# Sliding-window attention with a gated feed-forward: where the wide tiles transpose q and k, and which engine takes one of the x differences

## The chip, the cores and the metric

The kernel runs on one core of a Trainium2 chip. The metric is the device time of one execution in microseconds (us); lower is better. TensorE, VectorE (DVE in the profile), ScalarE (ACT), GpSimd (POOL) and SyncE (SP) each work through their own instructions in program order and wait for each other by semaphores.

## The reference

```
# q, k, v: [8, 8, 576, 64]   (batch, heads, positions, head size)
scores = q @ k^T / 8
keep   = (0 <= i - j) & (i - j < 64)            # causal window of 64 positions
attn   = softmax(where(keep, scores, -1e9))
x      = (attn @ v) as [4608, 512]              # tokens x (heads * 64)
out    = (max(x @ w_gate, 0) * (x @ w_val)) @ w_out    # w_gate, w_val 512 x 1536; w_out 1536 x 512
```

## The kernel before

The 4608 tokens are cut into ten tiles. Tiles 0 to 3 have 384 tokens, tiles 4 to 9 have 512 and are called wide. All matrix products run in fp16 with fp32 sums. The attention of a tile is computed while the feed-forward of the tiles before it runs.

**The order.** A planner (`Weaver`) keeps a clock that the code moves on with each group of TensorE products, and a heap of small steps with due times. `W.at(t, fn)` puts a step on the heap, and `W.advance` emits all steps that are due. This happens while the program is built: it decides the order of the instructions on every engine, and on the chip each engine then keeps that order. A step that waits on the chip holds up whatever stands behind it on its engine.

**q and k.** Each group of nine 64-position windows is one batch of q, k and v. The kernel loads q and k of a batch with four GpSimd DMAs (`qk_load`, L175: k and q, two groups of four heads each) and turns each with one VectorE transpose of 32 x 32 blocks (`qk_trans`, L195) into `kT` and `qT`. There are two sets of `kT` and `qT`, used in turn, and one buffer for each of the four loads, so a load waits until the transpose of the batch before has read its buffer. `plan_batch` puts the loads and the four transposes (k, k, q, q) on the heap. Of the wide tiles, 4 to 8 begin a new batch each and tile 9 does not.

**Scores and values.** The scores of a wide tile are computed in two quads of four windows (`q_st`, products at L261), each with four exponentials on ScalarE (`q_exp`, L402) and four masks on VectorE (`q_mask`, L407, fp16 in SBUF). `values` multiplies by v (L436), and VectorE divides by the sums (`t_recip` L450, `t_norm` L455) and turns the result into `xt` (`t_turn`, L461).

**The first two products of a wide tile** (`fast_hidden`, L597) use seven block products P1 to P7 in place of eight. They need four differences of blocks of x, called `xc`, made by `x_form` (L473): n = 0 needs only the first half of the heads, n = 1 needs the result of n = 0, n = 2 stands alone, and n = 3 needs n = 1. GpSimd makes n = 0, 2 and 3, VectorE makes n = 1:

```
x, y = ((b12, b11), (b22, xc[:, 0]), (b22, b12), (b21, xc[:, 1]))[n]
(nc.vector if n == 1 else nc.gpsimd).tensor_tensor(xc[:, n], x, y, SUB)
```

The 12 blocks of 128 hidden columns are taken in three groups, which the text calls blocks 0, 1 and 2. Within a block ScalarE copies sums out of PSUM (`seed` L606, `snap` L616). VectorE makes two kinds of work: the gate product of a direct result (`mult`, L622) and the sums of two results (`add`, L633), always one for the gate side and one for the value side. GpSimd multiplies the summed pairs (L622 on POOL). The product P3 writes on in the PSUM bank that the sum for P7 has read, so TensorE waits there for L633. Each block has two direct gates and two pairs of sums.

**What follows a tile's hidden part.** `fast_output` runs the third product (L699) in four groups of 128 tokens. Ahead of the first two stand the values of the next tile, ahead of the last two the scores of the tile after that. `o_sb` goes out by SyncE DMAs (L706).

**Where the transposes are planned.** `ahead(t)` runs at the beginning of each tile. In a wide tile t it plans the batch for tile t + 3, with times counted from the expected end of tile t (`T + WIDE_T`): loads 12 us earlier, transposes at `SLOTS` behind it, so they fall into tile t + 1. The batch for tile 6 is planned in tile 3 in the same manner.

Of the kernel before, what the change touches and what calls it, by code (L numbers as in the profile page):

```python
# [15 lines left out]
SUB = mybir.AluOpType.subtract  # L16
# [31 lines left out]
def kernel(  # L48
# [10 lines left out]
    nc = tc.nc  # L59
# [13 lines left out]
    NS = 4  # L73
# [69 lines left out]
    def xt_tile(t):  # L143
        if t not in xts:
            xts[t] = x_sb.tile([128, NC, WT], FP16, name="xt")
        return xts[t]
# [24 lines left out]
    def qk_load(b, name, hh):  # L171

        tile_ = nat[b, name, hh] = a_in.tile([128, S // 32 * D], FP16, name=f"{name}{hh}")
        src = (q if name == "q" else k)[b, G * hh:G * hh + G]
        nc.gpsimd.dma_start(tile_, src.rearrange("h (i j) d -> (h i) (j d)", i=32))  # L175
# [14 lines left out]
    def qk_trans(b, name, hh, j0=0, j1=S // 32):  # L190

        src = nat[b, name, hh].bitcast(FP32).rearrange("p (j e) -> p j e", e=32)
        dst = qTs[b % 2][:, hh] if name == "q" else kTs[b % 2][:, hh, 64:64 + S]
        dst = dst.bitcast(FP32).rearrange("p c o -> p (c o)")
        nc.vector.transpose(dst.rearrange("p (i j) -> p j i", i=32)[:, j0:j1], src[:, j0:j1])  # L195
# [36 lines left out]
    def one_bank():  # L232
        taken["one"] += 1
        to = singles[(taken["one"] - 1) % 4]
        while id(to) in unread:
            W.pop()
        return to

    def two_banks():
        taken["two"] += 1  # L240
        at = 4 + 2 * ((taken["two"] - 1) % 2)
        to = singles[at:at + 2]
        while any(id(one) in unread for one in to):
            W.pop()
        return to
# [141 lines left out]
    def q_window(qd, i):  # L387
        return NS * TT // 64 + QW * qd + i
# [21 lines left out]
    def scores(qd, T, banks=None, give=True):  # L410

        W.clock += q_st(qd, banks)
        for g in range(G):
            W.at(T + 0.8 + 0.6 * g, lambda g=g: q_exp(qd, g, give))
            W.at(T + 1.5 + 0.6 * g, lambda g=g: q_mask(qd, g))
# [50 lines left out]
    def x_form(t, n):  # L466

        if t not in xcs:
            xcs[t] = x_sb.tile([128, 4, 2, HT], FP16, name="xc", tag="xt")
        xt, xc = xt_tile(t), xcs[t]  # L470
        b11, b12, b21, b22 = (xt[:, 2 * k:2 * k + 2, HT * h:HT * h + HT] for k in range(2) for h in range(2))
        x, y = ((b12, b11), (b22, xc[:, 0]), (b22, b12), (b21, xc[:, 1]))[n]
        (nc.vector if n == 1 else nc.gpsimd).tensor_tensor(xc[:, n], x, y, SUB)  # L473
        if n == 3:
            normed[0] = t

    def values(t, hh, T, banks=None):

        t_pv(t, hh, banks or [bank() for _ in range(3)], banks is None)
        W.clock += 0.62  # L480
        W.at(T + 0.7, lambda: t_recip(t, hh))
        for i, k in enumerate((2, 0, 1)):
            W.at(T + 1.2 + 0.5 * i, lambda k=k: t_norm(t, hh, k))
        W.at(T + 2.7, lambda: t_turn(t, hh))
        for n, x in (((0, 4.0),), ((1, 4.0), (2, 4.1), (3, 5.0)))[hh]:
            W.at(T + x, lambda n=n: x_form(t, n))

    def w_form(wt, n, j):

        to = us if wt is wg else vs  # L490
        c = slice(256 * j, 256 * j + 256)
        f = slice(256 * j + 128 * HF, 256 * j + 128 * HF + 256)
        a11, a12, a21, a22 = wt[:, 0:2, c], wt[:, 2:4, c], wt[:, 0:2, f], wt[:, 2:4, f]
        x, y, op = ((a21, a22, ADD), (to[:, 0, :, c], a11, SUB), (a11, a21, SUB), (a12, to[:, 1, :, c], SUB))[n]
        nc.gpsimd.tensor_tensor(to[:, n, :, c], x, y, op)

    def plan_batch(b, load, trans):
        for i, (name, hh) in enumerate((n, hh) for n in "kq" for hh in range(2)):
            if load is not None:
                W.at(load, lambda name=name, hh=hh: qk_load(b, name, hh))  # L500
            W.at(trans[i], lambda name=name, hh=hh: qk_trans(b, name, hh))

    def plan_exps(T, u, mask=True, gap=0.4, first=0.8):
# [258 lines left out]
    with tc.manual_schedule():  # L762
# [85 lines left out]
        def pair(t, TA, TB, P):  # L848
            for u, T in ((2 * t, TA), (2 * t + 1, TB)):
                W.at(T, lambda u=u: u_st(u))  # L850
                plan_exps(T, u)
            W.at(P, lambda: u_pv(2 * t) + u_pv(2 * t + 1))
            for n in range(2):
                u = 2 * t + n
                W.at(P + 0.7 + 1.7 * n, lambda u=u: u_recip(u))
                for hh in range(2):
                    W.at(P + 0.9 + 0.5 * hh + 1.7 * n, lambda u=u, hh=hh: u_norm(u, hh))
                W.at(P + 1.9 + 1.7 * n, lambda u=u: u_turn(u))

        def loads(t, T):  # L860
            for u in (2 * t, 2 * t + 1):
                b, uu = divmod(u, UB)
                if uu == 0:
                    plan_batch(b, T - 12.0, (T - 1.5, T, T + 2.4, T + 4.8))
                W.at(T - 6.0, lambda u=u: v_load(u))
                W.at(T + 1.0, lambda u=u: v_spread(u))
# [5 lines left out]
        WIDE_T = L_T + 13.1  # L872

        def batch_of(t):
            w0 = q_window(2 * (t - NS), 0)
            b = (w0 + 2 * QW - 1) // NG
            return b, w0 <= NG * b

        def qk_ahead(t, T, gaps, lead=12.0):
            b, new = batch_of(t)  # L880
            if new:
                plan_batch(b, T - lead, [T + x for x in gaps])

        def v_ahead(t, T):
            b, new = batch_of(t)
            us = list(range(UB * b, UB * b + UB)) if new else []
            if t == NS:
                us.insert(0, UB * b - 1)
            for i, u in enumerate(us):
                W.at(T - 5.0, lambda u=u: v_load(u))  # L890
                W.at(T + 6.0 + 2.5 * i, lambda u=u: v_spread(u))

        LAST = NS + NL - 1
        SLOTS = (0.2, 3.4, 7.6, 13.8)

        def ahead(t):
            T = W.clock
            if t + 1 < NS:
                pair(t + 1, T + 8.5, T + 11.5, T + 17.3)
            if t == NS - 2:  # L900
                qk_ahead(NS, T + 20.5, (0.0, 1.5, 3.0, 4.5))
                v_ahead(NS, T + 20.0)
                for j in range(NF // 4):
                    for n, at in enumerate((0, 1, 3, 2)):
                        W.at(T + (1.0, 16.5, 22.9)[j] + 1.6 * n, lambda at=at, j=j: w_form(wv, at, j))
            if t == NS - 1:
                qk_ahead(NS + 1, T + 7.0, (0.0, 3.5, 4.7, 12.0), 6.0)
                for qd, x in ((0, 3.0), (1, 6.4), (2, 19.0), (3, 22.0)):
                    def st(qd=qd):
                        scores(qd, W.clock, two_banks() + two_banks(), qd == 3)  # L910
                    W.at(T + x, st)
                for hh in range(2):
                    def pv(hh=hh):
                        values(NS, hh, W.clock, two_banks() + [one_bank()])
                    W.at(T + 14.2 + 0.1 * hh, pv)
                qk_ahead(NS + 2, T + 27.6, SLOTS, 6.0)
                v_ahead(NS + 1, T + 27.6)
            if NS <= t:
                if t + 3 <= LAST:
                    qk_ahead(t + 3, T + WIDE_T, SLOTS)  # L920
                if t + 2 <= LAST:
                    v_ahead(t + 2, T + WIDE_T)

# [4 lines left out]
        T = 67.0  # L928
# [8 lines left out]
        for t in range(2, NS):  # L937
            ready(t)
            ahead(t)
            hidden(t, ((0, widths[t]),), each=4)  # L940
            output(t)
# [4 lines left out]
        for t in range(NS, NS + NL):  # L946
            ready(t)
            ahead(t)
            fast_hidden(t)
            between = [[] for _ in range(4)]  # L950
            if t + 1 <= LAST:
                between[0].append(lambda: values(t + 1, 0, W.clock))
                between[1].append(lambda: values(t + 1, 1, W.clock))
            if t + 2 <= LAST:
                for qh in range(2):
                    between[2 + qh].append(lambda qh=qh: scores(2 * (t + 2 - NS) + qh, W.clock))
            if t == LAST:
                fast_output(t, between[:-1])
                W.drain()
                output_last(t)  # L960
            else:
                fast_output(t, between)
# [31 lines left out]
```

## Time and profile before

| | |
|---|---|
| median of 3 runs | 318.36 us (318.19 to 318.55) |
| the profiled execution | 318.42 us |
| its span, first to last instruction | 316.7 us |
| TensorE busy | 302.8 us, 96% |
| VectorE busy | 225.6 us, 71% |
| ScalarE busy | 180.4 us, 57% |
| GpSimd busy | 160.5 us, 51% |
| granted TensorE clock | 1.00 |
| first wide tile (4) begins its products | 123.05 us |

In the profile, a group line gives the source line, engine, operation, result and inputs, shapes and count; behind the bar the busy time and the mean of one in ns, then the idle time of the engine just before and what ended it. A chain line gives a start, a length and a step. A timeline line gives a start, a length, the engine and the instructions merged into it; times in both are counted from the start of the span.

### The profile page before, as it was taken

What the parts mean: (1) busy time and instruction counts of PE and PEld (TensorE: products, weight loads), DVE (VectorE), ACT (ScalarE), POOL (GpSimd) and SP (SyncE); (2) the same over time, 40 slices, a digit from 0 to 9 for tenths busy, and PEclk for the clock granted to TensorE, in tenths of its full rate; (3) what the DMA queues carried; (4) which work ended last, traced back from release to release, by engine and by line L of the source; (5) the groups of instructions that cost most, each with busy time, mean ns of one, the idle gap of its engine ahead of it and who ended that gap; (6) DMA issues with size and microseconds to landing.
All of it is one profiled execution on the core that took longest, in us unless ns stands there. A gap on an engine that the chain in (4) does not pass through costs nothing.

```text
span 316.7 us, 10123 instructions
## 1 busy us (share of the span) xinstructions
PE 302.8 (96%) x4295; PEld 210.5 (66%) x4295; DVE 225.6 (71%) x413; ACT 180.4 (57%) x364; POOL 160.5 (51%) x178
## 2 busy tenths in 40 slices
PE   4899989999999998999999999999999999999995
PEld 2576947656646655885588458854887488748854
DVE  6937982787895886889876986699378937854540
ACT  3644324534526626882788267845885588518842
POOL 8859799513972019337814781347244404441430
PEclk9999999999999999999999999999999999999999
DMA  7999999929939216933990299002910210020002
GB/s 219 182 195 206 195 166 221 118 100 155 137 70 234 48 37 115 177 69 70 210 152 2 33 231 151 20 0 74 181 27 2 98 40 3 2 101 33 2 33 99
DMA packets 56748, 33.33 MB, mean 105 GB/s; under 512 B 39552, under 2 KB 48128, under 8 KB 56704
## 3 DMA queue, kind: packets, MB, share of 16 engines
q0 software_dynamic: 46688, 18.29, 49.8%
q1 hardware_dynamic: 9872, 14.34, 14.0%
q8 instruction: 33, 0.54, 0.7%
q14 instruction: 11, 0.09, 0.1%
q10 hardware_dynamic: 144, 0.07, 0.1%
HBM read 37.75 MB, written 9.44 MB: 149 GB/s over the span
## 4 chain that ended last, share of the span: by engine, by line
PE 84%; DVE 9%; ACT 3%; issue 1%; DMA 1%; POOL 0%; DVEq 0%; ACTq 0%
PE bank L597 30%; PE bank L699 19%; PE bank L554 19%; PE bank L714 7%; PE bank L261 3%; PE bank L436 2%; DVE kT L195 2%; DVE p L300 1%; PE bank L320 1%; DVE qT L195 1%; DMA vs<-in_k_dram 1%; DVE g_sb L622 1%; DVE pr L633 1%; PE bank L746 1%; ACT pr L616 1%
## 5 line engine op out<-in xcount | busy, mean ns | idle before, releaser
L622 POOL TENSOR_TENSOR g_sb<-pr 128x512 f16<-128x512 f32 x36 | 45.9, 1274 | 84.0 <-ACT pr L639 81.3
L699 PE MATMUL bank<-wo,g_sb 128*128 128x512 f16 x276 | 62.9, 380 | 0.0
L622 DVE TENSOR_TENSOR g_sb<-r,bank 128x512 f16<-128x512 f32 x36 | 24.7, 685 | 39.4 <-ACT r L650 25.8
L633 DVE TENSOR_TENSOR pr<-bank,pr 128x512 f32<-128x512 f32 x72 | 46.1, 680 | 2.4 <-PE bank L597 2.2
L616 ACT COPY pr<-bank 128x512 f32<-128x512 f32 x72 | 38.8, 595 | 11.8 <-PE bank L597 11.7
L699 PEld LDWEIGHTS <-g_sb 128*128 128x128 f16 x276 | 25.5, 98 | 28.9
L540 DVE TENSOR_TENSOR g_sb<-pr,bank 128x384 f16<-128x384 f32 x48 | 26.2, 549 | 22.0 <-PE bank L554 20.5
L537 ACT ACTIVATE pr<-bank 128x384 f32<-128x384 f32 x48 | 23.5, 494 | 24.8 <-PE bank L554 19.9
L554 PE MATMUL bank<-xt,wg 128*128 128x192 f16 (+1 forms) x256 | 34.8, 286 | 1.3 <-DVE xt L361 0.6
L201 POOL DMA_DIRECT2D v<-in_v_dram x41 | 34.7, 872 | 1.8 <-DMA q<-in_q_dram 1.0
L704 ACT COPY o_sb<-bank 128x512 f32<-128x512 f32 x23 | 13.5, 586 | 37.8 <-PE bank L699 32.3
L554 PE MATMUL bank<-xt,wv 128*128 128x192 f16 (+1 forms) x256 | 34.5, 286 | 0.0
L714 PE MATMUL bank<-wo,g_sb 128*128 128x512 f16 x144 | 32.8, 379 | 0.1
L597 PE MATMUL bank<-xc,us 128*128 128x256 f16 x216 | 32.4, 273 | 0.4 <-ACT pw L402 0.4
L597 PE MATMUL bank<-xc,vs 128*128 128x256 f16 x216 | 32.4, 273 | 0.3 <-ACT pw L402 0.3
L597 PEld LDWEIGHTS <-us 128*128 128x128 f16 x288 | 28.1, 98 | 6.7 <-issue 3.5
L597 PEld LDWEIGHTS <-vs 128*128 128x128 f16 x288 | 28.1, 98 | 4.6 <-issue 1.3
L473 POOL TENSOR_TENSOR xc<-xt 128x512 f16<-128x512 f16 x12 | 13.9, 1161 | 31.8 <-DVE xt L461 31.8
L554 PEld LDWEIGHTS <-wg 128*128 128x128 f16 x256 | 22.9, 98 | 10.3 <-DMA wg<-in_moe_w_gate_dram 0.8
L554 PEld LDWEIGHTS <-wv 128*128 128x128 f16 x256 | 22.8, 98 | 8.0
L639 ACT ACTIVATE pr<-pr 128x512 f32<-128x512 f32 x36 | 22.9, 636 | 7.7 <-DVE pr L633 7.7
L402 ACT ACTIVATE pw<-bank 128x512 f16<-128x512 f32 x48 | 25.4, 604 | 3.3 <-PE bank L261 2.9
(77 smaller groups left out, 481.3 us busy)
## 6 DMA issues: line engine op xcount, KB each, us to landing
out_dram<-o_sb SPq DMA_DIRECT2D x35, 256.0 KB, 3.3
k<-in_k_dram POOLq DMA_DIRECT2D x15, 288.0 KB, 5.4
q<-in_q_dram POOLq DMA_DIRECT2D x15, 288.0 KB, 7.8
v<-in_v_dram POOLq DMA_DIRECT2D x31, 128.0 KB, 6.5
v<-v SPq DMA_DIRECT2D x14, 132.0 KB, 3.3
v<-v SPq DMA_DIRECT2D x28, 66.0 KB, 3.0
wg<-in_moe_w_gate_dram POOLq DMA_DIRECT2D x6, 256.0 KB, 6.6
wv<-in_moe_w_val_dram POOLq DMA_DIRECT2D x6, 256.0 KB, 8.2
```

Of the source, the lines that this page charges most:

```text
L201: nc.gpsimd.dma_start(v16s[b % 2][lo:hi, g, :, 0:64], v[b, :, 64 * g - 64 + lo:64 * g - 64 + hi].rearrange("h p d -> p h d"))
L402: nc.scalar.activation(d["p"][g].rearrange("p n c -> p (n c)"), d["st"][g], ACT.Exp, scale=scale)
L537: nc.scalar.activation(part(r_sb), part(h1), ACT.Relu)
L540: nc.vector.tensor_tensor(g_sb[:, f:f + w, c0:c0 + n], part(r_sb), part(h2), MUL)
L554: nc.tensor.matmul(h[:, b * n:b * n + n], wt[:, c, (f + b) * 128:(f + b) * 128 + 128], xt[:, c, c0:c0 + n], start=(c == 0), stop=(c == NC ...
L597: nc.tensor.matmul(to[:, HT * m:HT * m + HT], w[:, k, 128 * m:128 * m + 128], x[:, k], start=(first and m == 0 and k == 0), stop=(k == 1), ...
L616: nc.scalar.copy(pr[:, i], at[j, "A", i])
L622: eng.tensor_tensor(gh[:, f:f + 2, h], pair(r), pair(v), MUL)
L633: nc.vector.tensor_tensor(pr[:, i], to, pr[:, i], ADD)
L639: nc.scalar.activation(pr[:, 0], pr[:, 0], ACT.Relu)
L699: nc.tensor.matmul(op, g_sb[:, f, 128 * sub:128 * sub + 128], wo[:, f], start=(i == 0), stop=(i == NF - 1))
L714: nc.tensor.matmul(op, g_sb[:, f, bass.ds(sub * 128, 128)], wo[:, f], start=(f == 0), stop=(f == NF - 1))
```

## The change

Three things are edited. First, all four differences of `x_form` are made by GpSimd. Second, the loads and the transposes of a batch are planned apart: `qk_loads` plans the loads at the time that they had before, and `qk_turns`, called at the beginning of wide tile t, plans the transposes of the batch for tile t + 2 from that tile's own beginning. Third, the offsets are new. Tiles 5 and 6 put both k transposes at the beginning, one q transpose behind the sums of block 0 and one behind those of block 1. Tile 4 has later offsets, so that its transposes stand at the beginning and behind the sums of blocks 0, 1 and 2, one at each place. The order of instructions on TensorE, ScalarE and SyncE stays as it was.

```diff
@@ x_form
-        (nc.vector if n == 1 else nc.gpsimd).tensor_tensor(xc[:, n], x, y, SUB)
+        nc.gpsimd.tensor_tensor(xc[:, n], x, y, SUB)
@@ plan_batch
             if load is not None:
                 W.at(load, lambda name=name, hh=hh: qk_load(b, name, hh))
+            if trans is None:
+                continue
             W.at(trans[i], lambda name=name, hh=hh: qk_trans(b, name, hh))
@@ ahead
-        SLOTS = (0.2, 3.4, 7.6, 13.8)
+        SLOTS = (0.1, 1.4, 8.0, 14.2)
+
+        def qk_loads(t, T):
+            b, new = batch_of(t)
+            if new:
+                plan_batch(b, T, None)
+
+        def qk_turns(t, T, slots=SLOTS):
+            b, new = batch_of(t)
+            if new:
+                plan_batch(b, None, [T + x for x in slots])
...
-                qk_ahead(NS + 2, T + 27.6, SLOTS, 6.0)
+                qk_loads(NS + 2, T + 21.6)
                 v_ahead(NS + 1, T + 27.6)
             if NS <= t:
+                if t + 2 <= LAST:
+                    qk_turns(t + 2, T, (3.6, 8.0, 14.2, 18.6) if t == NS else SLOTS)
                 if t + 3 <= LAST:
-                    qk_ahead(t + 3, T + WIDE_T, SLOTS)
+                    qk_loads(t + 3, T + WIDE_T - 12.0)
                 if t + 2 <= LAST:
                     v_ahead(t + 2, T + WIDE_T)
```

## The prediction

> **What bounds the kernel now.** I read the page first, then the chain that ended last in order of time, then the timeline of the wide tiles, then the groups of the instructions that the change moves.
>
> ```profile
> span 316.7 us, 10123 instructions
> PE 302.8 (96%) x4295; PEld 210.5 (66%) x4295; DVE 225.6 (71%) x413; ACT 180.4 (57%) x364; POOL 160.5 (51%) x178
> PE 84%; DVE 9%; ACT 3%; issue 1%; DMA 1%; POOL 0%; DVEq 0%; ACTq 0%
> ```
>
> TensorE is busy 96% of the span, so only TensorE's gaps can be won. VectorE (DVE) is the one other engine with a share of the chain that matters. Where DVE enters it, the chain in order of time tells:
>
> ```profile
> 160.37 0.69 DVE g_sb L622
> 161.06 1.17 DVE kT L195
> 162.23 0.53 DVE pr L633
> 162.76 0.04 issue
> 162.80 9.94 PE bank L597 x88
> ...
> 173.36 0.30 DVE qT L195
> 173.66 0.79 issue
> 174.45 0.69 DVE pr L633
> 175.15 0.04 issue
> 175.19 1.19 PE bank L597 x8
> ...
> 223.00 18.34 PE bank L597 x168
> ```
>
> This is wide tile 5. Twice a 1.25 us transpose of k or q (L195) stands in DVE's order between a gate product (L622) and the block's first sum (L633), and TensorE's product P3 (L597) waits for that sum. Tile 6 shows the same pair at 194.33 and 206.63. Tile 7, the last line, has no transposes, and its 168 products run without a step of another engine. The timeline gives the length of both stages, from the first product of the tile to the first values product (L436) of the next:
>
> ```profile
> 156.33 0.60 PE L597 MATMUL bank<-xt,wg 128*128 128x256 f16 x4
> ...
> 176.31 0.69 PE L436 MATMUL bank<-v,pw 128*32 128x65 f16 x64
> ```
>
> ```profile
> 222.84 0.60 PE L597 MATMUL bank<-xt,wg 128*128 128x256 f16 x4
> ...
> 241.27 0.69 PE L436 MATMUL bank<-v,pw 128*32 128x65 f16 x64
> ```
>
> Tile 5 takes 19.98 us, tile 6 (189.59 to 209.58) 19.99, tile 7 18.43. Tile 4 takes 19.93 (123.05 to 142.98), for partly other reasons. Last, the instructions that move:
>
> ```profile
> L195 DVE STREAM_TRANSPOSE kT<-k 128x576 f32<-128x576 f32 x16 | 19.7, 1243 | 0.2 <-ACT k L188 0.2
> L473 POOL TENSOR_TENSOR xc<-xt 128x512 f16<-128x512 f16 x12 | 13.9, 1161 | 31.8 <-DVE xt L461 31.8
> L473 DVE TENSOR_TENSOR xc<-xt,xc 128x512 f16<-128x512 f16 x6 | 8.4, 1403 | 0.7
> ```
>
> **The change, part by part.** TensorE, ScalarE and the DMA queue of SyncE keep their order; only DVE and GpSimd (POOL) change.
>
> *Tiles 5 and 6, transposes.* DVE's order was masks, k, gate, k, sum, sum ... gate, q, sum, sum. It becomes masks, k, k, gate, sum, sum, gate, sum, sum, q, gate and so on, with the second q behind the last sum of block 1. No transpose stands between a gate and its sums any more. That removes both gaps: 162.00 to 162.80 and on to 163.40, where 0.44 each is the undisturbed step, is 0.36 and 0.16; 173.88 to 175.19 and on to 175.78 is 0.87 and 0.16. The sum is 1.55, which is also 19.98 less 18.43. Tile 6 gives 1.56. Together 3.11 us.
>
> What hides them at the new places? The k pair follows the last mask (ends 156.37) and lasts 1.17 + 1.25, to 158.8. The gate behind it starts at 160.37, when ScalarE is done; DVE sat idle 2.84 us there. The first q keeps its place: in tile 7 the idle time there is 1.13 us (before 232.63), so at most 0.12 hangs over, and the sum behind it is ready 1.1 us before P3 asks (233.93 against 235.06). The second q goes where tile 7 shows DVE idle 1.76 us (before 238.75), which takes 1.25. If a cover were gone, the overhang beyond 0.59 us would reach TensorE: in tile 7 the sum ends at 228.32, P3 starts at 228.95, and 0.04 goes to the hand-over. Nothing else is late next, since tile 7 has no TensorE wait in this stage.
>
> *Tile 4, transposes.* The first k moves from between gate (128.07) and sum (129.93) to behind the last mask, the second k stays behind two sums, both q stand behind sums. TensorE's gap at that first sum goes: 129.76 to 130.50 and on to 131.10 is 0.30 and 0.16, together 0.46. The other gaps of tile 4, before 124.48 and 125.40, wait on ScalarE's exponentials; 1.03 us stays. But here k is loaded late, see the first rival.
>
> *The difference n = 1.* Six instructions of 1.40 us leave DVE, six go to GpSimd. GpSimd rows of this operation take 1.15 to 1.27; I take these ends, so GpSimd's chain n = 1, 2, 3 lasts 3.5 to 3.8 us. Before, it was 2.8 from the first difference behind the turn to the end of n = 3 (150.93 to 153.71). So everything behind it in GpSimd's queue comes 0.7 to 1.0 us later: the v loads behind four of the six chains and, in tile 4, four k and q loads ahead of them. The products that read the differences come much later: in tile 5 n = 3 ended at 153.71 and the first product with xc starts at 157.20. The v loads serve values some 20 us on. Cost on the path: nothing.
>
> On DVE the removal frees one thing on the path. In tile 4 the last q transpose of tile 5's batch waits behind this difference (118.80 to 120.17), and the scores at 121.40 wait 0.20 us for it. It will start at 118.66, behind the turn, and end by 119.9, before the scores begin at 120.32. They still stop at 120.80 for ScalarE. Gain 0.20, bounds 0 and 0.4.
>
> *Masks and GpSimd.* A mask takes 0.41 us, but the one that met the last GpSimd difference took 1.37: it waited until that was done. With three differences in a row there is more to meet. The strictest case is that GpSimd and the eight masks share no moment: 150.93 + 3 x 1.27 + 8 x 0.42 = 158.1 in tile 5 and 183.47 + 7.2 = 190.6 in tile 6. The k pair then ends at 160.5 and 193.1, against gates at 160.37 and 193.64: 0.15 late at most, inside the 0.59. The other end is no loss at all. I take nothing. [...]
>
> **Sum.** 3.11 + 0.46 + 0.20 = 3.77 us. The profiled execution took 318.42 (span 316.7 and 1.7 around it), so 314.65; it stands 0.06 above the median of 318.36, so 314.6.
>
> **Rivals.**
>
> *k lands late in tile 4 (other side).* The first k transpose of tile 4 now heads DVE's queue before the gate. Its load was issued at 121.35 and landed 4.1 us later; it will be issued at about 122.3 and land at 126.4, just before the last mask ends (126.6). Until 127.3 its start costs nothing (128.07 less 1.17 plus 0.59 less the 0.20 won above); from there each us is one on TensorE, since gate and sums queue behind it. Against it: the four k loads of tiles 4 and 5 landed in 4.1 to 6.5. For it: the q loads of the same queue took 7.8 to 9.4, and an output transfer and the v loads run beside it. At 6.5 the start is 128.8, 1.5 late, and the time 318.36 - 3.77 + 1.5 = 316.1. It decides from a landing of 8.8 (start 131.1); at 9.4 the start is 131.7, 4.4 late: 319.0.
>
> *GpSimd's DMA issues hold the masks too.* If the five v issues (4.3 us) behind the differences also kept masks out, the pair would come 3.7 us late in tile 5 and 3.0 in tile 6: 321.3; a third of that, 316.8. Against it: in tile 5 masks ran at 0.41 beside these issues.
>
> *The longer GpSimd chain reaches the products.* Six tiles with 0.7 to 1.0 more are 4.2 to 6.0, so 318.8 to 320.6. Against it are the 3.5 us of slack above; it decides only if a chain of 3.8 became one of 7. [...]
>
> *The gaps come back elsewhere.* If the transposes were only standing in for another wait of P3, the time would stay within 0.6 of 318.4. Against it is tile 7.
>
> *More is won.* If in tile 4 ScalarE's exponentials also fall into place, up to 1.03 more: 313.6.
>
> **Chances.** Forecast 0.72, with a range of its own of 314.0 to 315.3. Late k 0.08 at the partial size and 0.04 on the slower side. Held masks 0.06, at the partial size. Chain reaching the products 0.02. Gaps that come back 0.04. More won 0.04. This kernel's measurement can tell about 0.2% (0.64 us) from no change. Faster: 0.72 + 0.08 + 0.06 + 0.04 = 0.90; within 0.2%: 0.04; slower: 0.04 + 0.02 = 0.06. The range from 313.9 to 316.6 holds the forecast, most of the late k and a part of the held masks, and leaves out less than 0.2.
>
> **What would show it.** In the profile of the changed kernel, the stages of tiles 5 and 6 last 18.4 to 18.5 us, no chain step of L195 lies inside them, DVE's share of the chain falls by about 2 points, and GpSimd's L473 groups count 24 with 1.15 to 1.3 us each. In tile 4 the first k transpose starts by 127.3 less the shift and no wait on the sum is left. I am wrong if tiles 5 and 6 still show a TensorE gap before P3, if masks end after 158.7 in tile 5, or if DVE is found waiting for a DMA at the first k of tile 4.

## The result, and the profile after

| | before | changed |
|---|---|---|
| median, same chip | 318.46 us (4 runs) | 315.33 us (4 runs) |
| ratio | | 0.9904, 95% interval 0.9887 to 0.9921 |
| profiled execution | 318.42 us | 315.17 us |
| its span | 316.7 us | 313.5 us |

Forecast were 314.6 us, with a range of its own of 314.0 to 315.3, and 313.9 to 316.6 in all. The median lies inside the wide range and 0.03 us above the narrow one. The interval of the ratio stands for a gain of 2.5 to 3.6 us; the forecast gain of 3.77 us lies just outside it. In a second set of runs on another chip the changed kernel had a median of 314.96 us and a ratio of 0.9883 (0.9847 to 0.9919), a gain of 2.6 to 4.9 us, which holds the forecast. In what follows line numbers are those of the changed kernel: L599 is the wide tiles' product (L597 before), L624 the gate product (L622), L635 the sum (L633).

The page of the changed kernel, span, busy times and the shares of the chain that ended last:

```profile
span 313.5 us, 10122 instructions
PE 300.7 (96%) x4295; PEld 210.3 (67%) x4295; DVE 224.7 (72%) x407; ACT 180.1 (57%) x364; POOL 168.3 (54%) x184
PE 89%; DMA 3%; DVE 3%; ACT 2%; issue 1%; SPq 0%; DVEq 0%
```

VectorE lost six instructions and GpSimd won six, yet VectorE's busy time fell by only 0.9 us. Its share of the chain fell from 9% to 3%, where the prediction had about 2 points. The share does not measure the gain: from 100 us on, the steps of VectorE in the chain add up to 17.8 us before and to 0.6 us after, while the span fell by 3.2 us. Where TensorE waits, the chain goes back along the instructions of the engine that ended the wait, and those ran beside TensorE's products for the most part. In order of time, tiles 5, 6 and 7 now look the same in the chain:

```profile
156.36 18.34 PE bank L599 x168
...
188.08 18.34 PE bank L599 x168
...
219.77 18.34 PE bank L599 x168
```

All that TensorE's matmuls wait for from 100 us on, by what ended the wait (us in total, times, longest):

```profile
PE bank L599 <- ACT pw L402: 0.7, 2, 0.4
PE bank L261 <- ACT pw L402: 0.3, 1, 0.3
```

Before, this list had also 1.8 us on the sums and 0.2 us on the q transpose. Both lines are gone. The timeline shows where the k transposes went, in tile 4 and in tile 5:

```profile
127.68 1.26 DVE L195 STREAM_TRANSPOSE kT<-k 128x576 f32<-128x576 f32 x1 [0.81 <-DMA k<-in_k_dram]
...
128.78 0.68 DVE L624 TENSOR_TENSOR g_sb<-r,bank 128x512 f16<-128x512 f32 x1
...
129.39 1.27 DVE L635 TENSOR_TENSOR pr<-bank,pr 128x512 f32<-128x512 f32 x2
...
130.26 0.60 PE L599 MATMUL bank<-xt,us 128*128 128x256 f16 x4
...
150.77 5.56 DVE L407 TENSOR_TENSOR pw<-pw,mask 128x512 f16<-128x512 f16 x8 [0.28 <-ACT pw L402]
...
156.26 2.32 DVE L195 STREAM_TRANSPOSE kT<-k 128x576 f32<-128x576 f32 x2
...
160.24 0.69 DVE L624 TENSOR_TENSOR g_sb<-r,bank 128x512 f16<-128x512 f32 x1 [1.66 <-ACT r L652]
```

In tile 5 the pair ends at 158.6 and VectorE is idle for 1.66 us before the gate, as the prediction had it. In tile 4 VectorE did wait for k, 0.81 us. The prediction had named just this as a sign that it is wrong, and had asked for a start by 127.3 at the latest; it was 127.68. The first sum is done at about 130.1 all the same (the first half of the 1.27 us from 129.39), and P3 starts at 130.26 without a wait. So the sign came and the loss did not; the paragraph on the rivals tells why.

Where the 3.2 us of span came from, stage by stage. Each stage is a difference of two starts on TensorE, worked out from the trace of the one profiled execution of each kernel. Each ratio is to the kernel before on the same chip, which had medians of 318.46 to 319.09 us there, by fast runs alone. "Scores" reaches from the last scores ahead of tile 4 to its first product; "tile n" from a tile's first product to the next values product.

| kernel | scores | tile 4 | tile 5 | tile 6 | median | ratio to before (95%) |
|---|---|---|---|---|---|---|
| before | 2.73 | 19.93 | 19.98 | 19.99 | 318.46 | |
| changed | 2.37 | 19.47 | 18.43 | 18.43 | 315.33 | 0.9904 (0.9887 to 0.9921) |
| difference only | 2.37 | 19.92 | 19.98 | 19.99 | 318.40 | 0.9982 (0.9963 to 1.0001) |
| transposes only | 2.73 | 19.46 | 18.43 | 18.43 | 315.48 | 0.9897 (0.9867 to 0.9927) |
| k between again | 2.37 | 19.46 | 18.95 | 18.95 | 316.07 | 0.9907 (0.9882 to 0.9932) |
| q between again | 2.37 | 19.46 | 19.46 | 19.47 | 317.28 | 0.9947 (0.9927 to 0.9967) |
| k loads late | 2.37 | 27.59 | 18.43 | 18.43 | 322.64 | 1.0102 (1.0075 to 1.0128) |
| GpSimd reads | 2.37 | 19.46 | 20.10 | 19.38 | 317.43 | 0.9941 (0.9922 to 0.9960) |
| GpSimd writes | 2.38 | 19.46 | 18.43 | 18.43 | 315.39 | 0.9883 (0.9863 to 0.9903) |
| changed, again | 2.37 | 19.46 | 18.43 | 18.43 | 314.96 | 0.9883 (0.9847 to 0.9919) |
| early exponentials | 2.37 | 19.05 | 18.43 | 18.43 | 314.94 | 0.9876 (0.9844 to 0.9908) |
| ... and late copy | 2.37 | 18.95 | 18.43 | 18.43 | 314.32 | 0.9858 (0.9824 to 0.9891) |
| ... and early k | 2.37 | 18.43 | 18.43 | 18.43 | 313.96 | 0.9836 (0.9803 to 0.9869) |

A stage that no edit touches repeats to 0.01 us or so from kernel to kernel. The intervals of the ratios reach 0.5 to 1.2 us to each side, so smaller differences between two kernels are not told by the medians; the stages carry the readings below.

### The profile page after: what moved, and what is told of

The parts are those of the page before. It is cut to its first block, busy times and chain, and to the rows that moved or that the text cites. A ratio compares the mean times of both kernels' runs of the same rounds, so it can differ in the third digit from the quotient of the medians.

```text
span 313.5 us, 10122 instructions
## 1 busy us (share of the span) xinstructions
PE 300.7 (96%) x4295; PEld 210.3 (67%) x4295; DVE 224.7 (72%) x407; ACT 180.1 (57%) x364; POOL 168.3 (54%) x184
## 4 chain that ended last, share of the span: by engine, by line
PE 89%; DMA 3%; DVE 3%; ACT 2%; issue 1%; SPq 0%; DVEq 0%
PE bank L599 35%; PE bank L701 20%; PE bank L556 18%; PE bank L716 9%; PE bank L261 3%; PE bank L436 3%; DMA v<-v 2%; DVE qT L195 1%; PE bank L320 1%; DMA vs<-in_k_dram 1%; PE bank L748 1%; DVE kT L195 1%; DVE g_sb L542 1%; ACT pw L402 1%; ACT x L351 0%
## 5 line engine op out<-in xcount | busy, mean ns | idle before, releaser
L624 POOL TENSOR_TENSOR g_sb<-pr 128x512 f16<-128x512 f32 x36 | 45.9, 1275 | 73.3 <-ACT pr L641 72.6
L624 DVE TENSOR_TENSOR g_sb<-r,bank 128x512 f16<-128x512 f32 x36 | 24.8, 688 | 35.1 <-ACT r L652 24.2
L635 DVE TENSOR_TENSOR pr<-bank,pr 128x512 f32<-128x512 f32 x72 | 46.2, 683 | 2.9 <-PE bank L599 2.6
L407 DVE TENSOR_TENSOR pw<-pw,mask 128x512 f16<-128x512 f16 x48 | 29.2, 647 | 6.2 <-ACT pw L402 5.8
L599 PE MATMUL bank<-xc,us 128*128 128x256 f16 x216 | 32.4, 273 | 0.4 <-ACT pw L402 0.4
L599 PE MATMUL bank<-xc,vs 128*128 128x256 f16 x216 | 32.4, 273 | 0.3 <-ACT pw L402 0.3
L599 PEld LDWEIGHTS <-us 128*128 128x128 f16 x288 | 28.1, 98 | 3.9 <-issue 0.6
L599 PEld LDWEIGHTS <-vs 128*128 128x128 f16 x288 | 28.2, 98 | 3.8 <-issue 0.5
L473 POOL TENSOR_TENSOR xc<-xt 128x512 f16<-128x512 f16 x12 | 14.8, 1233 | 24.9 <-DVE xt L461 24.5
```

Source lines behind the costliest of these rows:

```text
L407: nc.vector.tensor_tensor(d["p"][g], d["p"][g], mask[:, None, :].to_broadcast([128, 2 * QW, 64]), MUL)
L599: nc.tensor.matmul(to[:, HT * m:HT * m + HT], w[:, k, 128 * m:128 * m + 128], x[:, k], start=(first and m == 0 and k == 0), stop=(k == 1), ...
L624: eng.tensor_tensor(gh[:, f:f + 2, h], pair(r), pair(v), MUL)
L635: nc.vector.tensor_tensor(pr[:, i], to, pr[:, i], ADD)
```

## The experiments

### Each half of the change alone

Difference only: the kernel before, with the one line of `x_form`.

```diff
-        (nc.vector if n == 1 else nc.gpsimd).tensor_tensor(xc[:, n], x, y, SUB)
+        nc.gpsimd.tensor_tensor(xc[:, n], x, y, SUB)
```

> The kernel before with only the x difference n = 1 moved to GpSimd; the transposes stay planned as before. My theory (the gain is made of separate gaps): only the gap at the scores of tile 4 goes, 0.2 to 0.4 us, so about 318.1; tiles 5 and 6 stay at 19.9 to 20.0 us, tile 4 keeps its waits on the sum. Rival (the freed DVE time carries the gain): 2 us or more faster, 316.4 or less. Rival (GpSimd is too slow for it): slower than 318.4 by 0.6 or more.

The scores stage fell by 0.36 us and no other stage moved. The median alone would not tell this from nothing (the interval ends at 1.0001). TensorE's waits from 118 to 212 us in this kernel:

```profile
PE bank L597 <- DVE pr L633: 1.8, 4, 0.7
PE bank L597 <- ACT pw L402: 0.7, 2, 0.4
PE bank L261 <- ACT pw L402: 0.3, 1, 0.3
```

All four waits on the sum are there still; only that on the q transpose is gone. The 8.4 us of VectorE time that the difference had taken bought 0.36 us.

Much of those 8.4 us was itself a wait for GpSimd, by an estimate from the next two lines and the masks. In the kernel before, VectorE's n = 1 started 0.02 us behind GpSimd's n = 2 and ended 0.28 us behind it, here for tile 5:

```profile
150.93 1.15 POOL L473 TENSOR_TENSOR xc<-xt 128x512 f16<-128x512 f16 x1 [0.78 <-DVE xt L461]
150.95 1.41 DVE L473 TENSOR_TENSOR xc<-xt,xc 128x512 f16<-128x512 f16 x1
```

A mask of the same size and with two inputs takes 0.41 us where it meets no difference. So, by this estimate, the change moved such a wait from n = 1 to the masks more than it freed VectorE; what n = 1 would take there alone, no run shows.

Transposes only: the changed kernel, with that line taken back.

> The changed kernel with n = 1 back on VectorE; only the transposes are planned anew. My theory: all gaps at the sums go (0.46 in tile 4, 1.55 each in tiles 5 and 6), the gap at tile 4's scores stays, so 0.2 to 0.4 slower than the changed kernel, 3.2 to 3.5 faster than before: about 315.0 to 315.6. In tile 4 the first k transpose starts about 1 us sooner than in the changed kernel (k is issued sooner). Rival (the transposes fit only because the difference left VectorE): the k pair ends behind the gate's time and half of the gain or more is lost, 316.9 or more.

The other share, to the hundredth: 2.73 us at the scores again, 18.43 in tiles 5 and 6, 19.46 in tile 4. So the k pair fits with the difference on VectorE too, and the rival that it does not falls. In tile 4 k had landed, and its first transpose started at 127.29 without a wait, though this run was 0.5 us later than the changed kernel at the tile's first product (123.62 against 123.11). The two halves are independent and add up.

### Which place costs what

The changed kernel, with one offset each.

```diff
-        SLOTS = (0.1, 1.4, 8.0, 14.2)
+        SLOTS = (0.1, 4.4, 8.0, 14.2)        # k between again
```

> The changed kernel with one offset changed, so that in tiles 5 and 6 the second k transpose stands between the first gate and the first sum again, as before. My theory: the first gap of each tile (0.36 and 0.16 on P3) comes back and nothing else: 1.0 us slower than the changed kernel, about 316.3; tiles 5 and 6 take 18.95. Rival (only the sum of transposes in a tile counts, not their place): same as the changed kernel, 315.3.

```diff
-        SLOTS = (0.1, 1.4, 8.0, 14.2)
+        SLOTS = (0.1, 1.4, 8.0, 15.8)        # q between again
```

> The changed kernel with one offset changed, so that in tiles 5 and 6 the second q transpose stands between the gate and the first sum of block 2, as before. My theory: the second gap of each tile (0.87 and 0.16) comes back: 2.1 us slower than the changed kernel, about 317.4; tiles 5 and 6 take 19.46. Rival (place does not matter): 315.3.

18.95 and 19.46 us, as forecast: 0.52 for the k transpose between gate and sum, 1.03 for the q transpose, twice each. The number of transposes in a tile is the same in all these kernels. In the medians of this set, against the kernel with GpSimd writes below (315.39 us, both tiles at 18.43), the two are 0.7 and 1.9 us slower, for 1.0 and 2.1 by the stages; the first of these is not clear of noise. In the second kernel the timeline of tile 5 shows the mechanism again:

```profile
172.33 1.25 DVE L195 STREAM_TRANSPOSE qT<-q 128x576 f32<-128x576 f32 x1
...
173.42 1.27 DVE L635 TENSOR_TENSOR pr<-bank,pr 128x512 f32<-128x512 f32 x2
...
174.16 0.60 PE L599 MATMUL bank<-xt,us 128*128 128x256 f16 x4 [0.71 <-DVE pr L635]
```

### The rival on the other side: k lands late in tile 4

The changed kernel, with the v loads ahead of the k and q loads in GpSimd's queue, in tile 4 alone.

```diff
-                qk_loads(NS + 2, T + 21.6)
                 v_ahead(NS + 1, T + 27.6)
+                W.at(T + 22.6, lambda: qk_loads(NS + 2, T + 22.6))
```

> The changed kernel with one thing moved: in tile 4 GpSimd issues the five v loads ahead of the four k and q loads, so k is issued about 4.2 us later. My theory: the first k transpose heads VectorE's queue, so beyond 127.8 us each us of its start is one on TensorE; k issued at 127.2 lands at 131.3 to 133.7, so the loss against the changed kernel is 3.5 to 5.9 us: 318.7 to 321.1, the whole gain or more. Rival (the block's work hides a late k, or the loads of k overtake): less than 1 us lost, below 316.4.

```profile
133.93 1.25 DVE L195 STREAM_TRANSPOSE kT<-k 128x576 f32<-128x576 f32 x1 [6.76 <-DMA k<-in_k_dram]
135.03 0.68 DVE L624 TENSOR_TENSOR g_sb<-r,bank 128x512 f16<-128x512 f32 x1
135.63 1.27 DVE L635 TENSOR_TENSOR pr<-bank,pr 128x512 f32<-128x512 f32 x2
...
136.36 1.01 PE L599 MATMUL bank<-xt,us 128*128 128x256 f16 x4 [5.63 <-DVE pr L635]
137.16 1.06 PE L599 MATMUL bank<-xt,vs 128*128 128x256 f16 x4
```

The mechanism is real: k, issued at 127.46, landed 6.4 us later, VectorE stood still for 6.76 us and TensorE for 5.63. This kernel is slower than the one before the change, ratio 1.0102. But tile 4 lost 8.1 us, not 3.5 to 5.9 (in the profiled execution, 323.35 us, the longest of the six). The rest comes after the wait. The next line gives a stretch and its length, the busy time of TensorE's matmuls, its weight loads, VectorE, ScalarE and GpSimd, then the clock that TensorE was granted, the share of the DMA engines and GB/s:

```profile
136.00:141.00 5.00, 4.64 (x22) 3.19 (x22) 4.04 (x6) 3.02 (x7) 1.26 (x1) 0.50 0.47 121
```

The granted clock was 0.50. As a sum, with 0.44 us for an undisturbed step of four products: 130.13 to 136.36 is 6.23 less 0.44, so 5.79 for the wait, and 136.36 to 141.31 is 4.95 for six steps of 0.44, so 2.3 for the clock. Together 8.1.

### Masks and GpSimd take turns

The changed kernel, with GpSimd instructions added behind n = 3 for tiles 5 and 6, once such as read SBUF (the engines' working memory), once such as only write it. Both write a tile that nobody reads any more.

```diff
         if n == 3:
             normed[0] = t
+        if n == 3 and t in (NS + 1, NS + 2):
+            for _ in range(4):                                    # GpSimd reads
+                nc.gpsimd.tensor_tensor(zero.rearrange("p (a n) -> p a n", a=2), b22, b12, SUB)
...
+            for _ in range(7):                                    # GpSimd writes
+                nc.gpsimd.memset(zero32.bitcast(FP16), 0.0)
```

> The changed kernel with four more differences on GpSimd into an unused tile, behind n = 3 for tiles 5 and 6 (about 5.3 us each; they add work, the result is the same). My theory (GpSimd instructions that read SBUF and masks take turns, one by one): four more masks take 1.3 us each, the k pair starts at about 160.2 in tile 5 and 191.1 in tile 6, the gate is 2.3 and 1.4 late, less 0.59 each: 2.5 us slower than the changed kernel, about 317.8. Rival (masks are held only by the first GpSimd instruction, or the pair's cover is larger): less than 0.5 slower. Rival (the later v loads are what costs): slower by the same amount as the next run.

> The changed kernel with seven fills on GpSimd at the same place in place of the four differences (they write SBUF and read nothing; 4 to 6 us for each tile, estimated from the fills of 64 and 128 columns that took 0.18 and 0.23 us). [...] Rival (any GpSimd work holds masks): about 2.5 slower, as in the run before.

VectorE in tile 5, first with the reads, then with the writes; and GpSimd with the writes:

```profile
150.60 9.40 DVE L407 TENSOR_TENSOR pw<-pw,mask 128x512 f16<-128x512 f16 x8 [0.29 <-ACT pw L402]
159.92 2.32 DVE L195 STREAM_TRANSPOSE kT<-k 128x576 f32<-128x576 f32 x2
162.09 0.67 DVE L627 TENSOR_TENSOR g_sb<-r,bank 128x512 f16<-128x512 f32 x1
```

```profile
151.39 5.75 DVE L407 TENSOR_TENSOR pw<-pw,mask 128x512 f16<-128x512 f16 x8 [0.28 <-ACT pw L402]
157.06 2.33 DVE L195 STREAM_TRANSPOSE kT<-k 128x576 f32<-128x576 f32 x2
```

```profile
154.94 5.50 POOL L478 MEMSET zero<- 128x768 f16 x7
```

With reads the eight masks last 9.40 us, the pair starts at 159.92, the gate is late, and tiles 5 and 6 lose 1.67 and 0.95 us, forecast 1.7 and 0.8. With 5.50 us of writes at the same place the masks last 5.75 us against 5.56 in the changed kernel, and both tiles stay at 18.43. So the four differences, which read SBUF, held the masks, and the seven fills, which only write it, did not. It is not GpSimd's time and not the v loads, which come later by about as much in both; the rival that any GpSimd work holds masks falls. The traces show the manner: one instruction of each engine in turn. In the changed kernel the masks of tile 5 range as follows (shortest, median and longest in ns):

```profile
L407 DVE TENSOR_TENSOR pw<-pw,mask x8: 414/416/1372, 150.8 to 155.9; 128x512 f16<-128x512 f16 x8
```

Three of the eight met a difference. They and the next one started 1.22 to 1.30 us apart; the last five started about 0.33 us apart.

### What is left of tile 4

The prediction kept 1.03 us of tile 4's gaps, on ScalarE's exponentials. Edits of ScalarE's order were tried on the changed kernel, which ran again beside them.

> The changed kernel again, unedited, beside the two versions below. Theory: 315.0 to 315.8. It also tells whether two places of its profile that are later than in the kernel before (0.40 us at the values products of tile 1 at 45 us, 0.24 at the second scores behind tile 4) come again (then they belong to the change) or not (then they vary from run to run).

The first place did come again. From the output products ahead of the values products of tile 1 to those behind them it is 5.45 us in the kernel before, 5.81 in the first profile of the changed one and 6.06 in this one. But all kernels of this study have the same program up to that point, and they range from 5.31 to 6.06 there, so it varies from run to run and does not belong to the change. It is a wait on the v spread (SyncE's transfer from v to v, L213) and on masks. The second place did not come again: the second scores behind tile 4 took 0.64 us as in the kernel before (0.87 in the first profile). That is a pause inside the products, put down to "issue": 0.49 us in the next run, nothing in most. Its cause is open.

```diff
-            W.at(T + 0.8 + 0.6 * g, lambda g=g: q_exp(qd, g, give))
+            W.at(T + 0.8 + gap * g, lambda g=g: q_exp(qd, g, give))      # gap: 0.1 in quad 3, else 0.6
```

> The changed kernel with the four exponentials of tile 5's second quad planned 0.1 apart in place of 0.6, so that on ScalarE they stand ahead of the copy of tile 3's last output, which waits for TensorE. Theory: in tile 4 the products before 124.5 and 125.5 wait for banks that these exponentials free; they go, but the first snapshot copy is about 0.4 late in their place: 0.5 us faster than the changed kernel, 314.8. Rival (the snapshot copies are the real limit there): no change, 315.3.

Tile 4 fell to 19.05 us, 0.41 of the 0.5 forecast. The median does not show it (314.94 against 314.96). The profiled execution had the pause of 0.49 us behind tile 4; whether the other executions had it is not known.

```diff
-        W.at(W.clock, evac)
+        W.at(W.clock + (2.0 if t == NS - 1 and sub == TT // 128 - 1 else 0.0), evac)
```

> As the run before, and the copy of tile 3's last output is planned 2 us later, so that on ScalarE it stands behind the two first snapshot copies. Theory: both gaps of tile 4 go, 0.9 us faster than the changed kernel: 314.4. Rival (the snapshots wait for something else): as the run before.

The time came out as forecast, 314.32 us for 314.4, but by luck: the changed kernel had 314.96 us in this set and not 315.3, so 0.64 us were won and not 0.9, and tile 4 shows 0.51 of it. The waits of tile 4's products on ScalarE are gone, and now the late k decides:

```profile
126.65 1.26 DVE L195 STREAM_TRANSPOSE kT<-k 128x576 f32<-128x576 f32 x1 [2.19 <-DMA k<-in_k_dram]
...
129.07 0.60 PE L599 MATMUL bank<-xt,us 128*128 128x256 f16 x4 [0.20 <-DVE pr L635]
```

Tile 4 takes 18.95, which is 18.43 and the 0.52 that a k transpose ahead of the first sum cost before. So the k loads were put ahead of the x differences, where GpSimd had been idle for 20 us:

```diff
-                qk_loads(NS + 2, T + 21.6)
+                b6 = batch_of(NS + 2)[0]
+                for name, at in (("k", 12.0), ("q", 21.6)):
+                    for hh in range(2):
+                        W.at(T + at, lambda name=name, hh=hh: qk_load(b6, name, hh))
```

> As the version with early exponentials and the late copy, and the two k loads of tile 6's batch stand ahead of the x differences on GpSimd (they were behind them), so that k has landed before tile 4 begins. In the run before, the first k transpose of tile 4 waited 2.19 us for its load and the first sum made TensorE wait 0.20 and 0.16 on P3. Theory: that wait goes, tile 4 takes 18.43 to 18.5 us (18.95 in the run before, 19.47 in the changed kernel): 0.5 us faster than the run before, about 313.8. Rival (the gap at the first sum has another cause): as the run before, 314.3.

```profile
119.66 4.93 DVE L407 TENSOR_TENSOR pw<-pw,mask 128x512 f16<-128x512 f16 x8
124.50 1.25 DVE L195 STREAM_TRANSPOSE kT<-k 128x576 f32<-128x576 f32 x1
126.72 0.69 DVE L624 TENSOR_TENSOR g_sb<-r,bank 128x512 f16<-128x512 f32 x1 [0.97 <-ACT r L652]
```

The transpose starts behind the last mask and is done a microsecond before the gate. Tile 4 takes 18.43 us like all others, and the only wait of a matmul that the profile names from 100 us on is 0.3 us at the scores ahead of tile 4. At 313.96 us, ratio 0.9836 (0.9803 to 0.9869), this version is faster than the kernel before. Against the changed kernel the stage shows 1.03 us; the interval of the ratio lies below that of the first set (0.9887 to 0.9921) and overlaps that of the second (0.9847 to 0.9919), and the two kernels were not run on one chip together.

## Why the prediction was right

**Tiles 5 and 6.** 3.11 us forecast, 1.55 and 1.56 measured. That the place makes the cost, and not the number, is shown by the two runs that put one transpose back: 0.52 and 1.03, the two terms of the sum. The covers held: 1.66 us idle are left before the gate of tile 5.

**Tile 4's sums.** 0.46 forecast, 0.46 measured (19.93 to 19.47).

**The q transpose at the scores.** 0.20 forecast with bounds 0 and 0.4, 0.36 measured, alone by the difference-only run. The term was too small because only the wait with a name was counted. Before, the scores stopped twice, at 120.80 for ScalarE and at 121.40 for the transpose; after, they stop once and run on from 121.22 in one piece. Besides the named wait of 0.20 us the second start is saved, 0.16 us. First the kernel before, then the changed one:

```profile
120.80 0.39 PE L261 MATMUL bank<-qT,kT 32*128 32x64 f16 x29 [0.28 <-ACT pw L402]
121.40 0.42 PE L261 MATMUL bank<-qT,kT 32*128 32x64 f16 x32 [0.20 <-DVE qT L195]
```

```profile
121.22 0.66 PE L261 MATMUL bank<-qT,kT 32*128 32x64 f16 x61 [0.27 <-ACT pw L402]
```

**The x difference.** 3.5 to 3.8 us were forecast for GpSimd's three differences; in tile 4 they took 3.75 (119.25 to 123.00). TensorE waited for none of them, as forecast. VectorE did wait, for the k loads that stand behind them in tile 4. VectorE was not freed by the whole 8.4 us: the masks of most tiles now meet two or three differences where they met one or none, and their busy time rose by 6.7 us (22.5 to 29.2). In tile 5 this cost nothing, since the masks catch up: they start 0.33 us apart and the exponentials ahead of them 0.48, and the k pair started at 156.26 against 156.29 before. The strictest case of the prediction, 158.1 for the end of the masks there, was too late by 1.8 us (it was 156.34): mask and difference together take 1.30 us, not 1.27 and 0.42, and masks in a row start 0.33 us apart, not 0.42. A difference took GpSimd 1.16 us where no mask ran (at 118.02), and a mask of that size took VectorE 0.41 where no difference ran, a factor of 2.8.

**The sum.** 3.77 us forecast; the four terms measured make 0.36 + 0.46 + 1.55 + 1.56 = 3.93. The profiled executions differ by 3.25, as the two places that vary from run to run happened to be 0.40 and 0.23 us longer in the changed kernel's. By the ratio, 3.77 in 318.4 is 0.9882; the two sets gave 0.9904 and 0.9883. That the second is so near to the forecast is chance, at an interval of 0.0036 to each side; what speaks for the sum are its four terms.

**The rivals.** The late k was near. The forecast had it issued at about 122.3 and landed at 126.4; it was issued at 122.95, landed 4.6 us later, and the transpose waited until 127.68. In the kernel without the difference on GpSimd it did not wait, so the wait is a cost of that part of the change. The limit of 127.3 was too strict by about 0.5, since 127.68 cost nothing and left 0.2. About half of this is the 0.20 that was taken off for an earlier tile, while the tile in fact began 0.06 later than before. The other half is a shorter way from transpose to sum: the gate started 1.10 us behind the transpose and the sum 0.61 behind the gate, for which the prediction had 1.17 and, by tile 7, 0.76. The prediction had not counted this cover, so that the late k cost nothing is in part luck. A us for a us beyond the limit was too low a price with k loads late: 8.1 us were lost there, 2.3 of them at a granted clock of 0.50. The forecast of 319.0 for the worst case counts the wait alone; what the clock does behind a wait of that length, no run shows. Held masks by DMA issues: refuted, masks ran at 0.41 beside them (154.58 to 156.34). (The price of that rival, 3.7 and 3.0 us, is 0.1 and 0.2 too low by the prediction's own rows: with the masks 4.3 us later the pairs end at 164.8 and 197.4, against gates at 160.37 and 193.64 and less 0.59 that is 3.8 and 3.2. It decided nothing.) The chain reaching the products, and the gaps coming back: refuted by 18.43. More won in tile 4: not by this change, but by the two edits of ScalarE's order and the early k loads.

## What to carry to other kernels

A step that is not urgent should stand behind the last instruction of a pair that somebody waits for, not between its two halves: the same 1.25 us cost 1.03, 0.52 or nothing by place alone, and a tile without the step shows where the idle time is to put it. Ahead of an in-order engine's queue such a step brings its own input onto the path, so look at where its load lands, and load earlier if another engine's queue delays the issue. Moving work off an engine is worth what waits behind it at that place (0.36 us here), not its busy time (8.4 us).

## What the runs showed of the hardware

With k loads late, TensorE ran at a granted clock of 0.50 for about 4.7 us (136.36 to 141.1) after 5.63 us without a product, which added 2.3 us to the wait; from 141 to 150 us the clock was 0.99. Four products of 256 columns started 0.85 us behind the four before, in place of 0.44. It is one run, and it does not tell how long a stop must be to bring this clock, nor what ends it.

Masks and GpSimd differences that met took turns, one instruction each, 1.30 us for the two. In tile 5 of the changed kernel both got longer by this: three masks took 1.29 to 1.37 us in place of 0.41, two differences 1.33 and 1.34 in place of 1.15. Seven fills on GpSimd, which read nothing, did not hold the masks beside them: the eight of tile 5 lasted 5.75 us against 5.56, and the median of the 16 masks of tiles 5 and 6 was 0.43 us, as in the changed kernel. With GpSimd reads that median was 1.37.
